# A searched order, sums and stores for pairs of token tiles, and an early sine in a fused FFN and long-convolution kernel

**Chip, cores, metric.** One core of a Trainium2 chip. Time is the device time of one execution in microseconds (us). The kernel before takes 190.48 us (median of 3 runs, 189.39 to 190.49).

## The reference

Input is x (2048 tokens by 640), k and v of the same shape, a 4-tap filter, a long filter of 2048 taps for each channel, and a feed-forward network (FFN) of width 1728. The result is x + s * g:

```python
def _A_ref(q, k, v, shift_k, ssm_k, ssm_D):     # s: a long convolution
    ...                                         # k_shift: 4 taps along the tokens
    kv = k_shift * v
    ...                                         # kv_f, kf_f: FFTs over 2*S samples
    y = ...                                     # irfft(kv_f * kf_f)[:S]
    y = y + kv * ssm_D[None, None, :]
    return q * y

def _B_ref(x, w1, b1, w2, b2):                  # the FFN
    h = _gelu(jnp.einsum("bsd,df->bsf", x, w1) + b1)
    return jnp.einsum("bsf,fd->bsd", h, w2) + b2

xn = _layernorm(A_q)
s = _A_ref(xn, A_k, A_v, A_shift_k, A_ssm_k, A_ssm_D)
g = _silu(_B_ref(xn, B_w1, B_b1, B_w2, B_b2))
return A_q + s * g
```

## The kernel before

The transforms are matrix products on TensorE. The first stage writes to DRAM (scrK, scrU). Twelve convolution units (six for each half of the channels) read a block of k and of u back, do the second stage, multiply, do the inverse's first stage into the tile of u, and store it (scrC). FFN matmuls fill the time between. All operations are listed once with what they depend on; a string, ORDER, gives the order in which they are issued, the engine of each (p TensorE, a ScalarE, d VectorE, g GpSimd, s SyncE's DMA queue) and the slot of each buffer.

```python
    def finish(j):                              # one token tile: sum and store
        op("fin", "DVE", lambda e: eng(e).tensor_tensor(out=xs(j), in0=xn[:, j, :], in1=xs(j), op=ALU.add),
           reads=[xn_b[j]], writes=[x_b[j]])
        op("store", "SP", lambda e: nc.sync.dma_start(out=out_v[:, j, :], in_=xs(j)), reads=[x_b[j]], size=160 * 1024)
    # ...
    uin_pool = Pool(vA_t + vB_t, [[vA_h]] * 2 + [[vB_h]] * 2)      # four tiles for u
    # ... in conv_unit(b, u):
        chain("uin", op("uin", "SP", lambda e: rd(scrU, uin), reads=scrU_b[b], writes=[uin], size=P * n * 2, extra=last("uin")))
        # ... s2k, s2u: second stage (L723); s2ev: evictions (L265); prod, comb: products on VectorE
        op("i1", "PE", i1, reads=[qb, tab_b], writes=pc)           # inverse, first stage (L755)
        # ... i1ev: evicted into uin.v
        op("cst", "POOL|SP", lambda e: dma(e)(out=by_n2(scrC)[:, b, k0:k1, :],
                                                        in_=uin.v[:, 0:n].rearrange("p (k d) -> p k d", d=H)),
           reads=[uin], writes=[scrC_b[b][u]], size=P * n * 2)
```

Unit 7's u can be read only when unit 3's result, which lies in the same tile, is stored. Other lines: L513 is the FFN's first product (f1), L576 its second (f2), L580 its silu, L610 the first transform stage, L777 the inverse's last stage, L559 the output store. In the changed kernel the numbers are 2 to 8 higher (L515, L584, L588, L618, L731, L763, L785, L564), and by one more where an experiment adds a line.

## Time and profile before

| | before (profiled execution) |
|---|---|
| span | 189.8 us |
| TensorE busy | 176.4 us (93%) |
| first real FFN matmul | 10.88 us |
| unit 3's, unit 6's, last unit's inverse | 116.8, 136.7, 160.4 us |
| last matmul, and the time from it to the end | 185.05 us, 4.75 us |

The rows to read are those of TensorE, which bounds the kernel: how much of a stretch it stands idle, what it waits for, and what clock it was granted. The prediction below shows these lines.

### The profile page before, as it was taken

The numbers are of one execution on the slowest core, as the hardware profiler recorded it, in microseconds if no ns is written. First come the engines' busy times: TensorE is split into PE (matmuls) and PEld (weight loads), VectorE is DVE, ScalarE is ACT, GpSimd is POOL, SyncE is SP. The second block draws the span as 40 slices with busy tenths as digits, with TensorE's granted clock in tenths as the row PEclk, the third lists the DMA queues.
The fourth block names the chain that finished last, engine by engine and source line by source line (L and its number), as shares of the span: only waits on it lengthen the run. The fifth ranks groups of instructions, "written<-read, shape, count | busy, mean of one in ns | idle before, by whom it ended". The sixth has DMA issues, their size and how long they took to land.

```text
span 189.8 us, 4770 instructions
## 1 busy us (share of the span) xinstructions
PE 176.4 (93%) x1907; PEld 92.2 (49%) x1907; DVE 164.6 (87%) x302; ACT 146.5 (77%) x225; POOL 20.6 (11%) x35
## 2 busy tenths in 40 slices
PE   7899999999898899999999999985999999989990
PEld 2285543345554465656433444332246565646660
DVE  6799979994799999999989999996498998669993
ACT  2899799797986999999999999994599987111110
POOL 4470410031021030000001100110010000000000
PEclk9999999999999999999999999996699999999997
DMA  5999969999999987898699998879762999568375
GB/s 141 350 418 414 408 200 348 323 310 379 384 333 328 234 282 206 155 293 252 137 298 286 243 380 256 240 192 327 215 207 50 342 303 337 157 214 338 107 260 191
DMA packets 44410, 51.44 MB, mean 271 GB/s; under 512 B 7442, under 2 KB 38547, under 8 KB 44388
## 3 DMA queue, kind: packets, MB, share of 16 engines
q1 hardware_dynamic: 43216, 47.03, 77.8%
q0 software_dynamic: 1024, 4.10, 6.4%
q8 instruction: 15, 0.25, 0.6%
q14 instruction: 7, 0.06, 0.1%
q10 hardware_dynamic: 148, 0.01, 0.1%
HBM read 31.47 MB, written 18.35 MB: 262 GB/s over the span
## 4 chain that ended last, share of the span: by engine, by line
PE 45%; DMA 29%; DVE 17%; ACT 4%; issue 2%; SPq 1%; POOLq 0%; ACTq 0%; DVEq 0%
PE ps L513 18%; PE ps L576 14%; DMA scrC<-v_all 9%; DMA mm<-scrC 7%; DMA kT<-in_x_dram 4%; PE ps L610 4%; DMA scrK<-mm 3%; PE ps L723 3%; DVE stats L383 3%; DMA v_all<-scrU 3%; DVE xn L784 2%; DMA x<-in_x_dram 2%; ACT mm L265 2%; DVE kT L557 2%; PE ps L777 1%
## 5 line engine op out<-in xcount | busy, mean ns | idle before, releaser
L513 PE MATMUL ps<-xnT,w_sb 128*128 128x512 bf16 (+1 forms) x280 | 64.5, 379 | 0.9 <-ACT sl L580 0.5
L576 PE MATMUL ps<-w_sb,hT 128*128 128x320 bf16 x432 | 63.6, 300 | 0.5 <-ACT sl L580 0.5
L576 PEld LDWEIGHTS <-hT 128*128 128x128 bf16 x448 | 41.8, 98 | 21.6 <-issue 5.8
L265 ACT CAST mm<-ps 128x640 bf16<-128x640 f32 (+1 forms) x62 | 39.4, 703 | 4.4 <-DMA scrK<-mm 3.3
L513 PEld LDWEIGHTS <-w_sb 128*128 128x128 bf16 x280 | 26.6, 101 | 31.4 <-issue 8.9
L265 ACT CAST v_all<-ps 128x960 bf16<-128x960 f32 (+2 forms) x38 | 33.4, 916 | 6.4 <-PE ps L723 4.1
L519 ACT ACTIVATE hT<-ps,b_f 128x512 bf16<-128x512 f32 (+1 forms) x56 | 36.9, 706 | 1.7 <-PE ps L513 1.2
L580 ACT ACTIVATE sl<-ps 128x320 bf16<-128x320 f32 x32 | 13.6, 445 | 21.1 <-PE ps L576 18.8
L784 DVE TENSOR_TENSOR xn<-ps,xn 128x640 bf16<-128x640 f32 x16 | 12.6, 817 | 3.8 <-PE ps L777 3.0
L736 DVE TENSOR_TENSOR kT<-v_all,k_all 128x960 bf16<-128x960 bf16 x16 | 9.8, 652 | 4.2 <-ACT v_all L265 4.2
L723 PEld LDWEIGHTS <-tabs 64*32 64x32 bf16 x704 | 7.6, 92 | 11.7 <-issue 7.3
L635 DVE TENSOR_TENSOR mm<-k_all,mm 128x2560 bf16<-128x2560 bf16 x8 | 11.8, 1480 | 0.1
L632 DVE TENSOR_TENSOR mm<-k_all,mm 128x2560 bf16<-128x2560 bf16 x8 | 11.8, 1478 | 0.0
L723 PE MATMUL ps<-v_all,tabs 64*32 64x240 bf16 (+1 forms) x352 | 9.0, 274 | 2.9 <-DMA v_all<-scrU 2.9
L265 DVE CAST v_all<-ps 128x960 bf16<-128x960 f32 (+1 forms) x8 | 8.6, 1070 | 2.1 <-PE ps L755 1.0
L383 DVE BATCH_NORM_STATS2 stats<-kT 128x6 f32<-128x320 bf16 x16 | 6.9, 472 | 3.8 <-DMA kT<-in_x_dram 3.8
L610 PEld LDWEIGHTS <-W 64*128 64x128 bf16 x128 | 4.5, 94 | 10.7 <-issue 8.0
L736 DVE TENSOR_TENSOR k_all<-v_all,xtra 128x960 bf16<-128x960 bf16 (+1 forms) x16 | 9.0, 609 | 0.1
L390 POOL TENSOR_TENSOR rstd<-veps,mhalf 128x4 f32<-128x4 f32 (+1 forms) x5 | 6.2, 1235 | 23.6 <-DVE veps L388 23.6
L265 ACT CAST k_all<-ps 128x960 bf16<-128x960 f32 x8 | 7.8, 977 | 0.4 <-PE ps L723 0.4
L582 DVE TENSOR_TENSOR xn<-xn,sl 128x640 bf16<-128x640 bf16 x16 | 7.7, 483 | 0.1
L265 DVE CAST k_all<-ps 128x960 bf16<-128x960 f32 x6 | 6.9, 1154 | 1.0 <-ACT v_all L265 0.8
(98 smaller groups left out, 200.7 us busy)
## 6 DMA issues: line engine op xcount, KB each, us to landing
mm<-scrC SPq DMA_DIRECT2D x8, 640.0 KB, 5.5
v_all<-scrU SPq DMA_DIRECT2D x10, 480.0 KB, 4.9
scrK<-mm SPq DMA_DIRECT2D x12, 320.0 KB, 3.8
scrU<-mm SPq DMA_DIRECT2D x12, 320.0 KB, 3.6
k_all<-scrK SPq DMA_DIRECT2D x7, 480.0 KB, 5.8
scrC<-v_all SPq DMA_DIRECT2D x7, 480.0 KB, 4.9
kT<-in_kT_dram SPq DMA_DIRECT2D x4, 640.0 KB, 10.6
v_all<-in_v_dram SPq DMA_DIRECT2D x4, 640.0 KB, 8.4
```

The costliest lines, as they stand in the source:

```text
L265: (nc.scalar.copy if e == "ACT" else nc.vector.tensor_copy)(out=out_, in_=in_)
L383: nc.vector.bn_stats(out=stats[:, j, h, :], in_=xs(j)[:, h * H:(h + 1) * H])
L513: nc.tensor.matmul(out=ps.v[:, lo * P:hi * P], lhsT=w1_sb[:, ft, t, :], rhs=xnT_b[c].v[:, t, lo * P:hi * P], start=(t == 0), stop=(t == DT ...
L519: op("gelu", "ACT", lambda e: nc.scalar.activation(out=hT_b[c].v[a:z, ft, :], in_=ps.v[a:z, :], func=ACT.Gelu_apprx_tanh, bias=b1_f[a:z, f ...
L576: nc.tensor.matmul(out=ps.v[:, 0:H], lhsT=hT_b[c].v[0:M, ft, q * P:(q + 1) * P], rhs=w[:, h * H:(h + 1) * H], start=(ft == 0), stop=(ft == ...
L580: op("silu", "ACT", lambda e, h=h, ps=ps: nc.scalar.activation(out=sl.v[:, h * H:(h + 1) * H], in_=ps.v[:, 0:H], func=ACT.Silu), reads=[ps ...
L610: nc.tensor.matmul(out=ps.v[:, h, 0:H], lhsT=W[r, j + t, :], rhs=src[r, b, j + t, :], start=True, stop=True)
L632: op("kv2", "DVE", lambda e: tt(out=kt_t, in0=win(0, 2), in1=wbc(0, 2), op=ALU.mult), reads=kb + [wb_b], writes=[kvt_b], extra=[u for b in ...
L635: op("kv2", "DVE", lambda e: tt(out=kt_t, in0=win(2, 2), in1=wbc(2, 2), op=ALU.mult), reads=kb + [wb_b], writes=[kvt_b])
L723: nc.tensor.matmul(out=ps.v[32 * g:32 * g + 32, r, i * w:(i + 1) * w], lhsT=F2[i][64 * r:64 * r + 64, :], rhs=part(src.v[64 * r:64 * r + 6 ...
L736: nc.vector.tensor_tensor(out=q[:, r], in0=uu[:, r, :, None, :].to_broadcast([P, 2, 2, w]), in1=ku[:, r, None, :, :].to_broadcast([P, 2, 2 ...
L784: nc.vector.tensor_tensor(out=xv, in0=ps.v[:, :, 0:H], in1=xv, op=ALU.mult)
```

## The change

The intent: fewer and larger sums and stores at the end, one activation-table load fewer at the start, and an order found by a search whose model had transfer times fitted to measured ones.

```diff
+NPAIR = 12
 ORDER = """
-1d 7p0 9s 1s 1s 1s -18p1 10g 1g -6p0 -7d 48d -27s 1s ...
+2d 5p0 -3p1 11a 53p0 -50s 1s 1s 1s 1s 5s 42a -58p1 -11d ...
 (the whole string is another one)
+    op("presin", "ACT", lambda e: nc.scalar.activation(out=acs[:, CH - 1, 0:1], in_=bias_pi[:], func=ACT.Sin), reads=[bias_b])
 ...
-    op("small2", "DVE", small2, writes=[sm_b], after=stat_ops)
+    op("small2", "DVE", small2, writes=[sm_b], after=stat_ops[:3])
 ...
-    def finish(j):
-        op("fin", "DVE", ...)
-        op("store", "SP", ...)
+    def finish(j, n):
+        x_, xn_, b = (xs2(j), xn[:, j:j + 2, :], x_b[j:j + 2]) if n == 2 else (xs(j), xn[:, j, :], [x_b[j]])
+        op("fin%d" % n, "DVE", lambda e: nc.vector.tensor_tensor(out=x_, in0=xn_, in1=x_, op=ALU.add), reads=xn_b[j:j + n], writes=b)
+        op("store", "SP", lambda e: nc.sync.dma_start(out=out_v[:, j:j + n, :] if n == 2 else out_v[:, j, :], in_=x_), reads=b,
+           size=n * 160 * 1024)
     def step_done(j):       (a pair is finished when both its tiles are)
```

In the new order, unit 3's store is also issued by SP where the old one had GpSimd's queue.

More of the change, by code (lines that the diff above doesn't have):

```diff
@@ L132 @@
 ORDER = """
-1d 7p0 9s 1s 1s 1s -18p1 10g 1g -6p0 -7d 48d -27s 1s 9d 1d 1d -24p1 -4p0 9a 23a -31p1 28g 5d -1d 2d 1g 3g 21p0 -2p1
--28d 1d 28a -22d 1d 6d 1d 17p2 -51g 52a -7p3 1a -38s -14p4 -7p5 63a -41s -14p4 -7p1 65p2 -46s 47a 22d -47d 27s 12p10
-2p0 2p2 -3a 2a 3p1 -1a -60s 62a -76d 36a 60p00 -18d -41a 200d 1d -227s 69d -1d 2d -13s 14g -51a -19s 227d 1d -142p3
--15d -70s 73d 11p2 4p 4a 9p1 -6p4 7a 9p5 -24p -16d 18p 2a 5a 13p6 -37d 14p2 13p1 11a 2a -12a -26d 23p0 60p60 1a 1p4
--113s 52a -8p -88s 92a 9p1 57a -53p0 -14a -48s 117p61 2p4 -3s 4a -2a -55a 120d -153p21 1d -24s 25p3 1d 3p4 -38d 39a
@@ L138 @@
--3p5 1d 24a 73p62 -25p23 1a 25d 51d -124p0 49p4 25p6 -24a 17p20 8a -133s 119g 7a -67a 75s -68p10 2p4 -1a 2a 1p5 50p61
-2p2 5p0 -43p4 109d 1d 1d 1d -75a 2a 5a -122s 80p6 -1a 10p22 2p0 -26a 11p4 115d 12d -122a 22s 15s -26a -91s -5s 90p5 4a
-3g 1p63 -17a 115d 12d -27p01 28d 1d 1d 1d -121a 132d -123p2 73s -72a -2a -100s 183a 42d -152p4 273d -271p2 270d -271a
-270d -273p3 5a 108p6 -91a 92a 29p02 -142a 31g 112a -126p2 1a 214p40 -78d 121d -41p5 -1a 2a -91p6 -82p03 2p2 81a -89g
-181p41 -123s 41d 121d -213a 24p60 149d -147p0 -24a 91d -9p21 -44s 212d -77a -148a 56s 251s1 -120g -189a 69d -91s 82a
@@ L143 @@
-91p5 -148s 149a -91p0 -18p62 2p2 17a -220s 202a 2a 1s 107p40 -74d -10p03 156d -163s 92a 73d -157a 256s0 -300p60 2p2 1a
-160d 3d -37p5 -128a 3g -104p4 145p0 3p22 78d -115p61 43d 110a 4s0 -38a -84a -34a 37a -159p5 165d 143d -142d -164p0
-155s 10d -156a 112p6 37p2 -36a 37a -158a 309d -144d -167a -75s 316p11 2p4 -119g 118a 70g -72d 4a -83s -100p60 30p23 1a
-182d 4s -27p00 -189a 190a -74d -92p41 2p2 191s -186p6 -4a 303s0 -116d -97d 134d -219a -201d 202s 220d -70d 1p11 71d
--137d -93a 227a -133d 137s1 -136d -116p22 -3p6 5p4 -1a 186p0 -189a 252d 77p2 2p6 -326a 178a 7a -60d 205p4 -216d 12d
@@ L148 @@
-60d -350p1 1d 164s 324a -146p0 73s 79a -204d 200a 1d1 13s1 -339p23 330p4 10p6 -162a 1d -53d -125a 189p10 141a 1d -313s
-322a -8d -142a -189p2 1a 324d -200d -122p42 2p6 121d 121s -255s 198p0 150p2 -334a 240s -242a 187a -54d 204a -9p64 2a
--1a -150p01 161p2 2p4 -235p61 73a -46d 47p1 160a 2a -235a 1p2 229d0 -156a -47d -44p40 2p6 17a -16a 250d -346s 247p00
-16p1 89s1 -227p23 2p6 -33d 154a 85s -128s 142d -221a 123p4 -111d 112a 91d -77a -58p00 -201s 349p2 -147a -79d -31s
-251p46 1a -210d 120p1 96a -242s 27d 120a 93s0 -3d -122p0 1a -100s 17p42 -5p60 7p2 203s -127p1 -77d 209p4 -207d 221s2
@@ L153 @@
--228a 215d -227p61 95a -93p2 -1a 2a 87p0 1a -71g 208d1 13s1 -228p6 -45p43 2p2 -1a 45d 215d -92p1 -166a 259p4 2p6 10p2
--162p0 178s0 -120a 95a 10a -12d 3d -250p42 2p6 -1d 96a -94a 109p1 1a -82g 244s2 -24d -541p0 550p2 1a -241s 244p6 2p4
--1d 27s1 -304s 279a -556d 448p1 1a 92p26 1a 9d2 1d -9a -93a -157s 272p4 -121p0 1a 112d -164p2 -4p3 178p6 4p0 -5d 7p4
--15d -164a -391p2 569d 10s3 -192a 178a -171p3 172d0 -565a 555p60 15a -13a -115p2 98s -146a 185p4 2p0 8s2 -146a 139a
--2a -24d 34s0 1p6 -20d -184p3 179d -8g 14d -216d 32a 219s0 -181p2 157d1 -10p04 1d 10d 8a 16s1 -33a -196p3 197g -149a
@@ L158 @@
-166p6 4p4 -3a 5p0 1a -220a 245s1 -242p2 243s2 -28d -3d2 1d 5d -16p64 2a -159p0 158a -202a 225p4 -180a 182p6 1a 3p2 1a
--180p1 152s 29p6 -185p0 186a -181a 173d -8d 25p4 16s2 -30d0 6d 25s3 -211a 170p26 25a -227p1 204a -1d -202a 22p0 1a
-204p4 4p2 2p6 -638p1 425p0 208a -10d -14g 30a -22d 20d 27s0 -238a -425d 633d1 6d -16p42 -174p61 176a -1a 23p0 2p2 4p4
--203a 200a -199p7 197d -8d 15p0 -292d 301s0 -13d2 -25s 28a -202a 204a 25s1 -47d 23d 8p2 1a -8d -204p60 -1d 250s0
--62p40 1d 25p2 15s1 -39a 25a 1d0 -213p7 215p0 -216a 218p2 10p4 -11a 26s1 -46d -188p61 210a 1d 33s2 -24a -227a 1d 235s3
@@ L163 @@
--49s 15p02 1a 10d 15p4 1a -25a 15d -210p7 1a 220d1 1d -11p04 2d -214a 197s -178p20 205p64 -11a 2s 14p0 -3a -1d 5d
--227d 18p3 1a -2a 211p4 1d 4p6 10p0 1d -20s 34s3 -24d -214d -9p31 1a 224p4 2p0 -7p6 -240p20 241d 9p6 -2d -2d 22p0 6p4
--5d 24s0 -23d 5d -274a 250d 21d 4d 4s1 -2d -276p2 1a 1d 250s2 -232p3 278p0 -19p4 6p6 -277p20 291d -24s -254a 248s
--247d 249s 9d 6d 16d -15d -4d 1s -31p0 6p4 18s 15p6 -4s 12d 1s -41d 43s -22d -271p3 244d 7d -6d 1s 1d 25s 7d 1s
--277p41 280d -284a 254d 1s -6s -244a -3a 1d 282d -32s 33s -280p2 1a 1d 279d 1s
+2d 5p0 -3p1 11a 53p0 -50s 1s 1s 1s 1s 5s 42a -58p1 -11d 13g -5p2 1p1 -8a 48d -24s 39p0 -32d 1d -21p1 -2p2 -7p1 62a
@@ new lines @@
+-27a -24g 48p2 -28d 6d -5g 4d 27p0 -25d -5d -30p1 10d 26g 25a -43s 13d 26a 13s -6p3 1a -66p1 38d 1d 1g -22s 27d 1d -5d
+50d -70s 68d -9p20 8d -6p3 -14s 13a 3p0 2p1 -3a 2a 22p20 -20a 21p3 -18d -42a -1a -5a 50d 35p0 -34g 155d -137p -17d 18p
+137d -121a -12a 15p1 -107s 99p4 -8a 17a 3p5 -2p6 1a -111s 2s 96p0 1a 14a -11p7 1a -57s 132p20 -5p01 6a -104d -1d 100d
+-78p6 -10p5 15a -52s 38p7 93p2 -83a -50s 101p02 33a -109d 4p41 1a 72a -69p6 102s -126s 94p2 -69a -8d 154d 1d -184d 46p
+4a -16p4 73a 1s 77d -150d 151d 11d -159p0 9p 4a 11p1 47p23 -98s 120p4 -92a 159d 1d 1d 1d 12d -102p6 -1a 22a 1g 69d
@@ new lines @@
+-90a 102d 1d 1d 1d 12d -159p00 -7a 50s -168g 143p2 -78s 61a 18a 5p3 25p40 -24a 26p6 -7p02 -24p2 32a -2a -44p3 -67s
+106a -24a 33p61 2p4 -34p0 -15a 50a -31p1 29a -32a 23p2 23p43 2p6 -55p0 37g 17a -62p4 19a 20a -19a 44a -70p5 56s -29p20
+2p6 -142s 128a -7p1 -1a 23a -2a 209p00 2p4 -238a 70s 75d 12d 1d 1d -114s 115d 1d -153a 99s 39p61 -32p23 123a -121p0
+56d -25a -30a 124p51 -150p62 24a 33p0 -118s 143d 66a 3a 78d -171a 91d 3p4 -108p20 -43a 82d -68s 171d -344s 311a -69d
+-57s -25p0 44p6 -1a 140d -30p50 71d -167s -56a 185d -141a 263s1 -154a 71d -151p23 -16p01 2p6 -250d 251a -59s -180p4
@@ new lines @@
+224s 139d 2d -32p5 -80a -252a 253p6 -50p22 33a -31p0 128a 70d -74d -75a -169p4 -67s 221g 7p60 159d -199a 42p0 117g 41g
+-151s -6d -45a 299s0 -408p5 152a -154p2 167d -46p61 2p0 191d -200s 65d -22s -164a 10a 239p31 2p4 -120a -2a 151d -148g
+-48p03 238d -314a 91p62 225a -149d 73d 78s0 -139d -254s 348d -93d 62a 2a 148s0 -147d 70d -223a 185s1 -31p20 -169a 104d
+-120p40 5p61 251d -239p0 198d -25p31 -4a -185a 120d 1d -116a 254s -242a -16p4 5p6 206a -22a -58d 126s -227p0 1a -30a
+1s 183p2 -179a 180a -169s 115d 198p0 2p4 4p6 -5a -141p3 -3d -54d 200a 1d1 13s1 -10a -146a 147p0 10p4 -13d 4a -307s
@@ new lines @@
+166p20 151a -93s -57a -7d 148d 1d -333p60 113p03 -111p4 1a 111a 71p31 149p40 1a -131d -78d -125d 335a 20s1 -170a -59d
+81s -21p2 -59d 81s -21a -356p4 1a 306d 203p6 4p0 -3a 4a 1p2 -4d1 -152p5 157a -220p62 1a -126s 189a 165p0 -8d -99p40
+94d 6d -236p2 244a -228p6 1a 75s 48p5 82s -221d 94p00 42a -253s 353p62 22s0 -118a -116d 214a -213d 70a 142d -220s
+128p1 1a -34p4 -213p20 2p6 117p01 133p5 -38a 128s0 -168d -47d -126a 339g -238g -99a 117d 59d -97p22 2p0 37p6 -117s
+249a -168d 37a 116p4 -155a 45d -313p5 314d 216p0 -222g 116a 110p6 2p2 -5a -84p4 -176s 266a -536d 534d 10s1 -230p03
@@ new lines @@
+247s2 -113a -55p5 54a -132d -28p20 2p6 105a -75p01 -29a 241d1 -148p4 -95d 244d -211p6 -5p2 4a -49p02 20s 93a 11p5
+-123a 1p0 49d 240s2 -25d -220a 228p6 2p2 -151a -122a 160p4 114a -2d -228g 117a 116p0 2p6 -15d 25p2 -11d 2a -116p5
+111d2 -10p06 2d 9d -275s 289a -161p4 162p2 -25a 29p0 2p6 -16d -116a -116s 256s1 -23d 24s3 -138p5 124a 1d0 3a -28s 30a
+-185p2 186d -130a -42p3 156p06 -153a -2a -17p4 206s0 -23d -142p3 132a -170a 204s0 -206a 173d 15d -14s 21p0 2p6 10p4
+16s2 -27d -150p2 152d 10a -9d1 25s1 -613p0 578p46 2d -150a -28p1 34a 143a 19p2 -597a 402a 186d 13p4 2p6 -5d 1d2 3a 2a
@@ new lines @@
+1d -163p0 164d -223p1 206p24 -146a -59a 207a 22p6 -23a -144p0 168a -34g 35p4 4p2 10s1 -29d 16d 5p6 -230p1 226d0 -25s
+-145a 175a -229p0 227a -13p46 11d -188p2 178d 22s2 17s0 -255a 2a 215a 14d 8p0 17s3 -16a 1p6 4p4 1a -14d -193a 203d
+-183p31 159s -158a 173p04 2d -1a -173p2 186p6 10p4 2p0 -197a 181d1 -179p30 184d -4d 5d 11a -2a 3d2 -196a 198p6 10s2
+-9a 1p0 10p4 -1s0 -211d 173s 30a -16d 26a -210p2 211p6 4p0 2p4 -16d 11d 1d0 12s1 17s0 -26a 10s1 -24d -201a 7p31 210a
+-22d -194d 225p0 10s1 10s2 -28d -34p64 67s3 -24a -8d -34a 1a -177p2 204d -205a 220p0 1a -42s 15p64 -192a 194a -1a 27d1
@@ L168 @@
+-25s -178p30 1a 192p04 11d -202p2 193a -1d -191a -19d 221p64 2d -1a -10s -192d 206p0 10p2 2p6 -11d -3s -213p41 1a 227d
+-2d 17s2 -11p0 -2p6 -228p5 215p2 14d 2d -11p6 -219a 217p0 -216d -24p40 238d 30p2 -27d 2d 21p0 -262p5 270s3 9s1 -4p6
+-8d -268a 272p2 -270a 262d 23p0 -278p41 256d 4d 8d -24s0 1p6 19d 15d -285d 7a 279d -11d 1s -21p2 8s 15p0 -7d 8d
+-268p40 1a -4p5 264s -16d -4d 15s -10d 30s -29s -5d -244a 245s -244d 270d 1s -268p4 275d 1s -275a 1d 267d 1s
 """
@@ L554, with xs2 @@
     left = {}
-    def finish(j):
-        op("fin", "DVE", lambda e: eng(e).tensor_tensor(out=xs(j), in0=xn[:, j, :], in1=xs(j), op=ALU.add),
-           reads=[xn_b[j]], writes=[x_b[j]])
-        op("store", "SP", lambda e: nc.sync.dma_start(out=out_v[:, j, :], in_=xs(j)), reads=[x_b[j]], size=160 * 1024)
-    def step_done(j):
-        left[j] = left.get(j, 3) - 1
-        if left[j] == 0:
-            finish(j)
+    def xs2(j):
+        return x01[:, j:j + 2, :] if j < 2 * CH else x23[:, j - 2 * CH:j - 2 * CH + 2, :]
+    def finish(j, n):
[3 more added lines that the diff above has]
+           size=n * 160 * 1024)
+    def step_done(j):
+        j0 = j - j % 2 if j < NPAIR else j
+        n = 2 if j < NPAIR else 1
+        left[j0] = left.get(j0, 3 * n) - 1
+        if left[j0] == 0:
+            finish(j0, n)
     def f2(c, q):
```

## The prediction

> **What bounds the kernel now.** I first read the page's busy times with the slices, then TensorE's waits, then the timeline round the longest wait, then the chain of waits, and last VectorE's timeline at the end.
>
> ```profile
> span 189.8 us, 4770 instructions
> ...
> PE 176.4 (93%) x1907; PEld 92.2 (49%) x1907; DVE 164.6 (87%) x302; ACT 146.5 (77%) x225; POOL 20.6 (11%) x35
> ...
> PE   7899999999898899999999999985999999989990
> ...
> PEclk9999999999999999999999999996699999999997
> ```
>
> TensorE (PE) is the bound: 176.4 of 189.8 us busy, and the change removes no matmul. So it can gain only in what is not full-speed matmul work: some 13 us without work, and the stretch where the clock row falls to 6, in the 28th and 29th slice (of 4.75 us each, so from 128 to 138 us). TensorE's own waits say where:
>
> ```profile
> PE ps L723 <- DMA v_all<-scrU: 2.9, 1, 2.9
> PE ps L311 <- DVE xtra L305: 1.3, 1, 1.3
> PE ps L777 <- DMA mm<-scrC: 1.2, 2, 0.8
> PE ps L610 <- DVE v_all L639: 0.9, 1, 0.9
> ```
>
> One wait of 2.9 us stands out: the second-stage transform (L723) waits for a block of u that is read back from DRAM into a tile of v_all. TensorE's timeline there:
>
> ```profile
> 127.20 0.40 PE L723 MATMUL ps<-k_all,tabs 64*32 64x240 bf16 x16
> 130.45 0.60 PE L723 MATMUL ps<-v_all,tabs 64*32 64x240 bf16 x16 [2.85 <-DMA v_all<-scrU]
> ...
> 131.38 2.32 PE L513 MATMUL ps<-xnT,w_sb 128*128 128x512 bf16 x5
> ...
> 134.16 2.26 PE L513 MATMUL ps<-xnT,w_sb 128*128 128x512 bf16 x5
> ...
> 137.22 1.04 PE L513 MATMUL ps<-xnT,w_sb 128*128 128x512 bf16 x4
> ```
>
> After it the groups of five L513 matmuls take 2.25 and 2.19 us in the chain where others take 1.13 to 1.19. So the wait costs twice: 2.85 us idle, then about 2 x 1.05 + 0.8 (the L723 groups) = 2.9 us of slow clock. What led to the wait is in the chain:
>
> ```profile
> 117.65 1.16 DVE v_all L265
> ...
> 118.84 0.48 issue
> ...
> 119.33 5.93 DMA scrC<-v_all
> ...
> 125.32 5.08 DMA v_all<-scrU
> ...
> 130.45 1.00 PE ps L723 x25
> ```
>
> There are four tiles for u. Unit 3 of the convolution writes its result over its u, stores it (5.93 us, from the POOL queue), and only then may the u of unit 7 be read into the same tile (5.08 us). From the start of unit 3's first inverse transform (116.84 us) to the u of unit 7 it is 13.6 us, and the order gives TensorE less than that to do.
>
> [...]The trace has eight loads of 1.28 us; at 12.03 us the sine activation starts right behind its load (13.32 us)[...]. [...]additions of 640 bf16 elements take 0.48 us and follow each other by 0.40 to 0.43, those of 1280 take 0.82 and follow by 0.69 to 0.73. [...]The output stores of 160 KB land after 1.9 to 2.2 us[...].
>
> **The change part by part.** *Sums and stores for pairs.* Tiles 0 to 11 are summed and stored two at a time: 16 sums become 6 of 1280 elements and 4 of 640, and 16 stores become 10. VectorE saves 12 x 0.42 - 6 x 0.72 = 0.7 us, and SP six issues of 0.33 to 0.5 us. All of it is after 171 us, where VectorE hardly rests (7.70 of 8 us in the stretch 172 to 180) and stays a step behind TensorE. The last links stay, for the last tile is still single:
>
> ```profile
> 185.73 0.48 DVE L582 TENSOR_TENSOR xn<-xn,sl 128x640 bf16<-128x640 bf16 x1
> 186.25 0.49 DVE L557 TENSOR_TENSOR kT<-xn,kT 128x640 bf16<-128x640 bf16 x1
> ```
>
> TensorE ends at about 185.1 us and the kernel at 189.8: silu, product, sum and the last store keep these 4.7 us. I count 0.3 us for less VectorE backlog.
>
> *Sine table first.* A one-element sine is put ahead of the first statistics on ScalarE. [...]the load at 12.03 us goes: 1.28 us of ScalarE. But TensorE does not wait for ScalarE between 11 and 22 us (11.00 of 11.00 busy[...]), so this shortens a backlog and not the end. The new order puts one or two evictions of the weight rows before ScalarE's statistics, in time it now waits for x (2.21 us), of the five between 7.11 and 9.53 us, so the transposes' evictions and the first real matmul (10.88 us) may come 0.3 us earlier. If instead the load sits behind the first of these evictions it delays the statistics by about as much. I count 0.3.
>
> *Order.* I counted the blocks of work on TensorE in both orders, and priced them from the trace (L513 group 1.14, L576 group 2.01, L723 group 0.33, inverse 0.61, L465 group 0.33). From unit 3's inverse to unit 7's u, the old order has six L513 groups, seven L723 groups and three inverses: 6 x 1.14 + 7 x 0.33 + 1.5 = 10.7 us. The new one has seven L513 groups and one L465 group besides: 12.1 us. And unit 3's store moves from the POOL queue to SP, without the 0.48 us of issue and nearer the 4.9 us median of SP's stores: the need falls from 13.6 to about 12.5. So the wait falls from 2.85 to about 0.5: gain 2.3 us. With it the slow clock should go in most runs. In the profiled execution it cost 2.9 us; but that one took 191.6 us, and the three timed ones had a median 1.1 us below, so part of the spell was often absent: I take 1.3.
>
> Earlier, VectorE stood 3.78 us on the late second half of x before its statistics, and TensorE waited for it (the 0.9 above). The new order holds these statistics until more products of k and v are done: gain 0.9.
>
> Against this, new tight spots. From unit 4's inverse to unit 8's u the work stays 12.2 us, while the need is 12 to 13.6, and its store is still on POOL; before, the stall of unit 7 fell inside this stretch and covered it. The first tile of v's second half is free only 5.7 us of work before unit 4 needs its u, against 0.4 us of issue and the 4.9 us median landing. Units 9, 10 and 11 have 13.1, 13.4 and 14.5 us (13.7, 14.3 and 14.8 before). At the end, three L576 groups and the inverse transforms still cover about 9.3 us between the last unit and the first read of its results; so the 0.8 us wait there stays. I charge 1.0.
>
> Sum: 0.3 + 0.3 + 2.3 + 1.3 + 0.9 - 1.0 = 4.1 us; 190.48 - 4.1 = 186.4.
>
> **The rivals.** First, *the wait is moved, not removed*: unit 8, or unit 4, or the stores of the first half (ScalarE waits 3.3 us on scrK stores now) stop TensorE for 2 to 3 us, perhaps with another slow spell. For it: DMA is over 90% busy in many slices, and landings of one kind vary (the reads of scrU from 3.1 us up), so an order tuned to mean landings can miss. Against it: all four covers but the one named stay within 0.9 us of the old. That makes 188.5 to 190.5. Second, *the slow clock is a matter of phase*: any idle time can bring it, or the fast runs of before never had it. Then only idle time counts: 187.5 to 188. Third, *VectorE becomes the bound*: with TensorE some 4 us faster, VectorE's 164.6 - 0.7 us must fit into a shorter span (about 88%), and it follows rather than leads between 104 and 120 us, where it is already full (7.85 and 7.99 of 8 us). Against it, what it loses now (3.78 us for x, some 4 us round the big wait) comes back. That would make 187. A better case: with no wait left in the middle and no slow spell, 6 to 7 us fall, to 183.8.
>
> **Range and chances.** The limit of 2% is 186.67 us, close to my 186.4. The gain is one wait with its slow clock; if both go I am well under, if the order moves the wait I am over. There is nearly nothing that could cost 2%. I give 0.53 to faster, 0.45 to same and 0.02 to slower, and 183.8 to 189.4 as the range.
>
> **What would show it.** Right: TensorE's longest wait for v_all<-scrU under 1 us, the clock row without a 6, L513 groups of 1.2 us throughout, seven table loads and none at 12 us with the time at the first L513 matmul near 10.6, VectorE without a stop for x near 48 us, a busy time of VectorE lower by about 0.7 us, and TensorE's busy time lower by 1 to 3 us for the missing slow spell. Wrong: a new wait over 2 us of TensorE on scrU, scrC or ScalarE, a clock that falls anyway, or a start of the first L513 matmul after 11.5 us.

## The result, and the profile after

The changed kernel took **183.88 us** (median of 4 runs: 188.76, 183.26, 184.08, 183.69), the kernel before in the same rounds 190.49. The ratio is 0.964, with an interval of 0.956 to 0.972: faster. Ratios here are the mean time of one kernel's fast runs over that of the other's fast runs of the same rounds, so not quite the ratio of the medians. The profiled execution happened to be the slow one of the four. Its page, answering to the rows of before:

```profile
span 187.0 us, 4730 instructions
...
PE 174.6 (93%) x1894; PEld 92.4 (49%) x1907; DVE 165.7 (89%) x296; ACT 146.6 (78%) x226; POOL 17.8 (10%) x33
...
PE   6999999999999999999999999994999999996990
...
PEclk9999999999999999999999999998599999999999
```

The low clock is still there, in the 29th slice (0.50 from 129.4 to 136.2 us), behind a wait of the same kind. TensorE's timeline in that execution:

```profile
130.09 0.60 PE L731 MATMUL ps<-v_all,tabs 64*32 64x240 bf16 x16 [2.52 <-DMA v_all<-scrU]
...
131.82 4.05 PE L515 MATMUL ps<-xnT,w_sb 128*128 128x512 bf16 x9 [0.34 <-issue]
```

A second execution of the same file was profiled in the fast state (span 183.0 us; experiment a_again):

```profile
128.65 0.40 PE L731 MATMUL ps<-v_all,tabs 64*32 64x240 bf16 x16 [1.85 <-DMA v_all<-scrU]
...
129.39 2.33 PE L515 MATMUL ps<-xnT,w_sb 128*128 128x512 bf16 x10
```

Read the two together: the wait for unit 7's u is there in both, 2.52 and 1.85 us, where I had expected 0.5. Behind it, nine matmuls took 4.05 us in the one, ten took 2.33 us in the other. (The x1894 of the page says that 13 matmul records are missing in that trace; the 0.34 us of "issue" goes with such a gap.) So the wait was made smaller but not removed, and the slow clock comes behind it in some executions only. Why the wait stays is in the chain of the first of the two:

```profile
116.18 0.62 PE ps L763 x16
...
118.86 5.70 DMA scrC<-v_all
...
124.58 5.46 DMA v_all<-scrU
```

From unit 3's inverse at 116.18 to the u of unit 7 at 130.04 it is still 13.9 us (13.3 in the fast execution, 13.6 in the profile of before). The store is on SP now, but took 5.70 us all the same, and it was issued no sooner after the inverse: 2.75 us behind the inverse's start (2.49 before). The timeline shows what it waited for:

```profile
117.33 0.40 DVE L753 TENSOR_TENSOR kT<-kT 128x480 bf16<-128x480 bf16 x1
...
117.64 1.15 DVE L266 CAST v_all<-ps 128x960 bf16<-128x960 f32 x1
...
118.86 0.36 SPq L774 DMA_DIRECT2D scrC<-v_all  x1
```

VectorE evicts half of the inverse's result. It was still at two sums of 0.40 us (L752, L753) when the inverse ended at 116.72, so its eviction ended only at 118.79, 0.07 us before the store. (The chain names two gelus of ScalarE at this point; the second ended at 118.95, after the store's issue, so it was not they.)

What became better lies elsewhere. The rows of time by stretch give, for each stretch, its length and the busy time of TensorE, then of weight loads, VectorE, ScalarE and GpSimd. Before:

```profile
34.00:50.00 16.00, 15.32 (x98) 7.28 (x96) 11.91 (x16) 14.21 (x24) 2.09 (x3) 1.00 0.98 347
50.00:64.00 14.00, 12.58 (x93) 7.08 (x91) 13.76 (x30) 11.53 (x21) 1.88 (x2) 1.00 0.97 321
```

And in the fast execution of after:

```profile
34.00:50.00 16.00, 16.00 (x107) 7.86 (x105) 15.59 (x16) 14.86 (x25) 0.69 (x1) 1.00 0.97 329
50.00:64.00 14.00, 13.61 (x100) 7.36 (x97) 13.69 (x36) 12.71 (x22) 2.73 (x3) 1.00 0.98 326
```

VectorE is busy 15.59 of 16 us where it was 11.91, and TensorE's idle time in the two stretches falls from 2.10 to 0.39 us. VectorE's stop in the timeline of before has no counterpart after:

```profile
48.53 0.89 DVE L383 BATCH_NORM_STATS2 stats<-kT 128x6 f32<-128x320 bf16 x2 [3.78 <-DMA kT<-in_x_dram]
```

The 6.8 us between the two profiled spans (189.8 and 183.0) split, by TensorE's idle time in each stretch and the length of its matmul groups, as follows: 2.9 the slow spell of before; 1.1 less wait between 120 and 131 us; 1.8 less idle from 22 to 64 us; 0.7 in 112 to 120 and 152 to 163; 0.85 at the start (next paragraph); minus 0.5 in 163 to 172 us, before the inverse's last stage; minus 0.2 from the last matmul to the end (5.0 against 4.8 us); the remaining 0.2 I don't place.

The start: in the first 11 us TensorE's idle time fell by 0.5 us, but its first FFN matmul came only 0.05 us earlier (10.83 and 10.88). What counts is when the clock becomes full. The first matmuls of 256 columns follow each other by 0.213 us up to 13.4 us in the profile of before, and by 0.109 from there; in the fast execution of after the step comes at 11.7 us. That is 1.7 us less at half speed. It differs between executions of one file, too (13.4 in the slow profile of after), so it is no merit of the change.

The early sine did not save a load. ScalarE's timeline after:

```profile
2.03 1.28 ACT L266 ACT_TABLE_LOAD   x1 [2.03 <-issue]
...
3.93 1.28 ACT L304 ACT_TABLE_LOAD   x1
```

The first eviction loads a set, and the sine behind it loads its own; the load at 12.03 us is gone, so there are eight as before. The first L515 matmul begins at 10.89 us (10.83 in the fast execution; 10.88 before).

### The profile page after: what moved, and what is told of

Same layout as the page of the kernel before. It is cut to its first block, busy times and chain, and to the rows that moved or that the text cites. A ratio compares the mean times of both kernels' runs of the same rounds, so it can differ in the third digit from the quotient of the medians.

```text
span 187.0 us, 4730 instructions
## 1 busy us (share of the span) xinstructions
PE 174.6 (93%) x1894; PEld 92.4 (49%) x1907; DVE 165.7 (89%) x296; ACT 146.6 (78%) x226; POOL 17.8 (10%) x33
## 4 chain that ended last, share of the span: by engine, by line
PE 69%; DMA 16%; DVE 7%; ACT 4%; issue 1%; SPq 1%; ACTq 0%
PE ps L584 28%; PE ps L515 21%; DMA w_sb<-in_w_dram 6%; PE ps L731 5%; PE ps L618 5%; DMA scrC<-v_all 3%; DMA v_all<-scrU 3%; PE ps L763 3%; DVE xn L792 3%; DMA mm<-scrC 3%; PE ps L313 2%; ACT mm L266 2%; DVE kT L563 2%; DVE x L563 2%; PE ps L480 1%
## 5 line engine op out<-in xcount | busy, mean ns | idle before, releaser
L515 PE MATMUL ps<-xnT,w_sb 128*128 128x512 bf16 (+1 forms) x267 | 62.6, 379 | 1.7 <-issue 1.1
L515 PEld LDWEIGHTS <-w_sb 128*128 128x128 bf16 x280 | 26.2, 102 | 31.6 <-issue 9.1
L266 ACT CAST mm<-ps 128x640 bf16<-128x640 f32 (+1 forms) x60 | 38.9, 709 | 2.2 <-PE ps L618 0.9
L266 ACT CAST v_all<-ps 128x960 bf16<-128x960 f32 (+2 forms) x32 | 28.8, 922 | 4.7 <-PE ps L731 3.2
L588 ACT ACTIVATE sl<-ps 128x320 bf16<-128x320 f32 x32 | 14.2, 449 | 21.5 <-PE ps L584 21.5
L266 DVE CAST v_all<-ps 128x960 bf16<-128x960 f32 (+2 forms) x14 | 15.1, 1082 | 6.4 <-PE ps L763 3.0
L266 ACT CAST k_all<-ps 128x960 bf16<-128x960 f32 x12 | 11.9, 988 | 1.0 <-PE ps L731 1.0
L744 DVE TENSOR_TENSOR k_all<-v_all,k_all 128x960 bf16<-128x960 bf16 x16 | 9.7, 652 | 1.4 <-ACT v_all L266 1.4
L618 PE MATMUL ps<-v_all,W 64*128 64x320 bf16 x64 | 7.8, 300 | 0.0
L266 DVE CAST mm<-ps 128x640 bf16<-128x640 f32 x9 | 7.4, 820 | 0.1
L744 DVE TENSOR_TENSOR kT<-v_all,k_all 128x960 bf16<-128x960 bf16 x12 | 7.2, 653 | 0.2
```

What stands on the lines that cost most here:

```text
L266: (nc.scalar.copy if e == "ACT" else nc.vector.tensor_copy)(out=out_, in_=in_)
L515: nc.tensor.matmul(out=ps.v[:, lo * P:hi * P], lhsT=w1_sb[:, ft, t, :], rhs=xnT_b[c].v[:, t, lo * P:hi * P], start=(t == 0), stop=(t == DT ...
L588: op("silu", "ACT", lambda e, h=h, ps=ps: nc.scalar.activation(out=sl.v[:, h * H:(h + 1) * H], in_=ps.v[:, 0:H], func=ACT.Silu), reads=[ps ...
L618: nc.tensor.matmul(out=ps.v[:, h, 0:H], lhsT=W[r, j + t, :], rhs=src[r, b, j + t, :], start=True, stop=True)
L744: nc.vector.tensor_tensor(out=q[:, r], in0=uu[:, r, :, None, :].to_broadcast([P, 2, 2, w]), in1=ku[:, r, None, :, :].to_broadcast([P, 2, 2 ...
```

## The experiments

In the order texts below, "f1#44" is the 45th operation of kind f1, and so on. Before took a median of 189.8 to 190.4 us in each of the five batches.

### Both kernels again

Edits: none.

> The kernel before, unchanged, to see the granted clock of each of its runs. Theory A (one wait of TensorE near 2.9 us for unit 7's u, and the slow clock it brings, make most of the change's gain): every run near 190.5 us has a mean clock near 0.98, that is, the slow spell is in all of them. Rival P (the slow clock is a matter of phase, and the kernel before has it as rarely as the kernel after): some runs have a clock of 1.00 and take about 187.5 us.

> The kernel after, unchanged. Theory A: most runs take 183.3 to 184.1 us at a clock of 1.00, and a run that has the slow spell again shows a clock near 0.98 and takes about 5 us more, near 188.8, because the wait and the spell come together. Rival P: clock and time are not tied; there are runs at 0.98 of 185 to 187 us.

b_again: 190.13 us (15 runs from 187.41 to 192.11, and two of 335 and 581 us that I leave out here; the median is over all 17), ratio 1.001. a_again: 184.57 us (184.07 to 186.61), ratio 0.971. Both are what they were. Theory A fails for the kernel before: its clocks reach from 0.959 to 0.997 in these runs, and in the same rounds one run at 1.000 took 189.33 us, where rival P had 187.5. For the changed kernel no run near 188.8 came; the one slow run, 186.61 at 0.988, lies where rival P put it. In b_again's profile TensorE waits 3.6 us for u; in a_again's it waits 1.9.

### Is it the wait for unit 7's u?

b_cover moves two groups of L513 in front of the wait, b_fill puts 12 useless matmuls there (their result is overwritten):

```diff
 order of before (b_cover)
+f1#44 (TensorE), f1#42 (TensorE)
 s2u#13            the one that waits for unit 7's u
 ...
-f1#44
-f1#42
```
```diff
 before (b_fill)
-                def s2(e, src=src, ps=ps, t=t):
+                def s2(e, src=src, ps=ps, t=t, fill=(nm == "s2u" and b == 1 and u == 1 and t == 0)):
+                    for _ in range(12 if fill else 0):
+                        nc.tensor.matmul(out=ps.v[:, 0, :], lhsT=w1_sb[:, 0, 0, :], rhs=flat(w1_sb[:, 0])[:, 0:512], start=True, stop=True)
```

> The kernel before with only this: two groups of five L513 matmuls (2.3 us) that followed the wait for unit 7's u now stand ahead of it. Theory A: the wait falls from 2.9 to about 0.6 us, the slow spell goes, clock 1.00: 190.5 - 2.3 - 2.9 = about 185.3 us. Rival R (the gain comes from the pairs, the table and VectorE's order, spread over the kernel): 189 to 190. Rival G (given back: what was moved is missing behind the wait, and TensorE stops there instead): 187.5 to 189.

> The kernel before with twelve needless 128x512 matmuls (12 x 0.216 = 2.6 us at full clock) into the bank of unit 7's first product, just ahead of it, so that the array works while the u is awaited. The wait for the u is not shorter. Theory A: no slow spell, clock 1.00, time falls by the spell alone, 2.9 us: about 187.6. Rival P (the spell isn't due to the idle time): clock still near 0.98, time 190.5 or a little more.

b_cover: 188.53 us (19 runs, 187.43 to 191.74); its ratio of fast runs, 0.999, says "same". b_fill: 188.80 us (4 runs, 186.07 to 189.61), ratio 0.982. In b_cover the wait for u fell to 0.23 us, but TensorE then stood 0.87, 0.26 and 0.47 us right behind it: the matmuls moved up were missing there. In both profiles the span was 186.2 to 186.3 us, with no slow spell. So the wait with its spell is worth some 3.5 us in an execution that has both, but only about 1.5 us in the median, for executions without the spell are common in the kernel before too. It alone doesn't make the change.

### A fifth tile for u

The table W of sines is needed for the last time by its four transposes (gtr). When all are done early, its memory can hold one more tile of u, and unit 7 need not wait for unit 3's store:

```diff
-    uin_pool = Pool(vA_t + vB_t, [[vA_h]] * 2 + [[vB_h]] * 2)
+    W_h = held([W_b])
+    uin_pool = Pool(vA_t + vB_t + [flat(W)[:, 0:UC]], [[vA_h]] * 2 + [[vB_h]] * 2 + [[W_h]])
 order: the last gtr and its eviction some 30 to 90 operations earlier; uin#7 into the new tile right behind uin#6;
 uin#8 to uin#11 each at the place of the one before
```

> The kernel after with a fifth tile for u: the weights W of the first stage are needed no more once they are transposed, so unit 7's u goes there at once, and each later u takes the tile that its forerunner had (the last W transposes moved ahead to free it). Theory A (reuse of the u tiles makes the wait): TensorE's wait of 1.9 us for unit 7's u goes to under 0.3, none of that kind takes its place, and no slow spell is seen: about 184.6 - 1.9 = 182.7 us. Rival G (given back: the products behind it or the read of the results stop TensorE for as long): 184 to 184.6.

> The kernel before with the same fifth tile and nothing else (the last W transpose moved ahead). Theory A: the wait of 2.9 us and the slow spell, found in about half of its runs, go: 190.1 - 2.9 - 1.3 = about 186 us, clock 1.00. If the order does the rest of the change's gain elsewhere, it stays 1 to 2 us above the kernel after (184.6). Rival G, as it was with the two groups moved: 188 to 188.5.

a_fifth: 183.63 us (182.60 to 183.88), ratio 0.969; no wait for u is left in TensorE's list. But of the 1.9 us only some 0.5 to 0.9 reached the end: the run lies between theory A's 182.7 and rival G's 184, and TensorE now waits 0.7 us for a block of k (L732) and 0.6 us for ScalarE (L467). b_fifth: 189.33 us over 16 runs (185.86 to 191.80), ratio of fast runs 0.985. The old order gains little in the median: its clocks still reach from 0.971 to 1.0, though the profiled execution had neither the wait nor a slow spell (184.2 us). What brings the low clocks in its other runs is not shown: none of them was profiled.

### The statistics alone

VectorE's stop for x, taken away in the old order: the statistics that wait go behind the last product of that part.

```diff
 order of before (b_stats)
-stats#9, stats#8, stats#7, stats#10, veps#3, pow#3 at their six places
 kv1#15
+stats#9, stats#8, stats#7, stats#10, veps#3, pow#3
```

> The kernel before, with only the statistics of the four tiles 8 to 11 moved back on VectorE, behind the next products of k and v, as the new order has it. If VectorE's 3.8 us stop for x at 45 to 48 us is worth what I predicted: VectorE has no stop for x, TensorE's waits near 58 us go, and the time falls by 0.9 to 1.8 us, to about 188.8. Rival: the wait further on takes it all up (TensorE only comes earlier to unit 7's u): within 0.4 us of the kernel before.

194.20 us (3 runs, 191.39 to 194.82), ratio 1.019, with an interval from 0.999 to 1.039: no gain, and probably slower. TensorE's waits show what took its place:

```profile
PE ps L513 <- ACT sl L580: 3.3, 1, 3.3
PE ps L723 <- DMA v_all<-scrU: 2.8, 1, 2.8
```

VectorE now waits 3.4 us for ScalarE and 2.2 us for x anyway, and TensorE stands 3.3 us for ScalarE with a slow spell behind (the mean clock of this execution is 0.973). So VectorE's stop can't be removed by that move alone, and the run doesn't tell what the stop itself cost.

### The pairs and the early sine

a_noparts has the new order with single sums and stores and no sine; a_nopairs has the sine; b_parts is the old order with both parts.

```diff
 after (a_nopairs)
-NPAIR = 12
+NPAIR = 0
 (a_noparts) as well:
-    op("presin", "ACT", ...)
 before (b_parts): the code of after, the old order, presin#0 ahead of asum#0 on ScalarE, each pair where its second tile was
```

> The kernel after in its own order, but without the other two parts: sums and stores tile by tile, each pair's in the place of the joint one, and no early sine. Theory O (the order makes the gain): 184.6 + 0.7 = 185.3 us at most. Rival R (pairs and table are worth 2 us or more): over 186.6.

> The changed kernel with its pairs undone and its early sine kept. Undoing both cost 2.0 us. Theory S: the pairs are most of it, through the seven single stores that SP issues one after another: 185.6 to 186.4 us, and 6.0 to 6.3 us from the last matmul to the end. Rival T (the early sine is most of it, by a faster start): 184.6 to 185.2, and about 5 us at the end.

> The kernel before with its old order, and only the two coded parts of the change: sums and stores for pairs, and the sine of one element ahead of ScalarE's first statistics. Theory S (the pairs only pay where SP's issues of the last stores end last, which they do in the new order and not in the old; ScalarE's early load is off the path): 189.3 to 190.3 us, ratio 0.993 to 1.003, time from the last matmul to the end 4.6 to 4.9 us. Rival P (the two parts are worth the 2 us that they were worth in the new order, whatever the order): 187.8 to 188.5, ratio 0.986 to 0.990.

a_noparts: 186.57 us (185.46 to 188.34), ratio 0.983. a_nopairs: 185.98 us (184.70 to 186.29), ratio 0.982. b_parts: 191.53 us (190.15 to 192.01), ratio 1.012, although its early sine did leave out a table load (seven in its trace). So the parts give nothing in the old order (if anything the reverse; three runs), and in the new order the pairs give most of what both give; between a_noparts and a_nopairs, with overlapping ranges, the sine shows no gain that three runs could settle. Where the pairs gain is seen in SP's timeline at the end of a_noparts (second column: time over all the issues of the group):

```profile
180.18 1.89 SPq L564 DMA_DIRECT2D out_dram<-x  x4
182.16 1.40 SPq L564 DMA_DIRECT2D out_dram<-kT  x3
```

and SP's of a_again:

```profile
178.15 1.83 SPq L564 DMA_DIRECT2D out_dram<-kT  x3
```

In a_noparts SP issues seven stores one behind the other, 0.47 us each, and is done at 183.56, 1.59 us after the end of VectorE's last sum (181.97). With pairs it is done at 179.98, 0.45 us after that end (179.53). From the last matmul to the end it is 6.2 us in a_noparts, 6.0 in a_nopairs and 4.5 to 5.0 in the four profiles of the changed kernel (4.8 before). In the kernel before, SP is 0.6 us behind VectorE (187.35 and 186.74) without any pairs, so there was nothing to gain. By the traces the pairs are worth 1 us or more, in SP's issues and not in VectorE's sums, and only where the order brings the last sums close together: they take back what the new order itself loses at the end. (The times of three runs each, from other rounds than the changed kernel's, would not show it by themselves.)

### Half of the order each

Up to about 66 us both orders have done nearly the same set of operations. h_early takes the new order (without the two parts) up to there and the old one for the rest, h_late the reverse.

```diff
 h_early: operations 1 to 315 of the new order, then what is left in the old order
 h_late:  operations 1 to 309 of the old order, then what is left in the new order
```

> A graft: the new order (without pairs and early sine) for the first 315 operations, up to some 66 us, then the old order for all that is left. Theory E (the gain of the new order in the first 64 us goes through to the end): TensorE idle 0.6 us or less between 22 and 64 us against 2.45 in the kernel before, the wait for unit 7's u stays near 3 us with the slow clock in part of the runs, 188.0 to 188.9 us, ratio 0.987 to 0.992. Rival M (the later DMA round trips set the time, and what comes early is waited away later): wait for unit 7's u over 4 us, 189.6 to 190.6 us.

> The opposite graft: the old order for the first 309 operations, then the new order (without pairs and early sine). Theory E (the middle is worth what its smaller wait and the missing slow spell give, 1.0 and about 1.5 us): 187.2 to 188.4 us, ratio 0.983 to 0.989, no slow spell, 6 us from last matmul to end. Rival (the new order gains only through its first 64 us): 189.6 to 190.6 us. A second rival (the whole gain is in the middle): 186.3 to 186.9, which is the changed kernel without its parts.

h_early: 189.57 us (19 runs, 188.31 to 190.84), ratio 1.001. h_late: 191.63 us (19 runs, 188.83 to 194.22), ratio 1.005. Neither half brings anything. For h_late the graft itself spoils the test: TensorE waits 1.9 us at the seam for ScalarE, the first transform stage ends at 110.4 us in place of 106.7, the wait for u is 2.9 us as before, and the clock in its profile is low a second time, from 8.2 to 11.6 us. h_early is clearer: TensorE's idle time from 22 to 64 us was 0.66 us (2.45 before), and unit 6's inverse came at 131.5 us (136.7 before, with the slow spell). But then:

```profile
147.31 0.60 PE L723 MATMUL ps<-v_all,tabs 64*32 64x240 bf16 x16 [2.43 <-DMA v_all<-scrU]
147.84 3.48 PE L576 MATMUL ps<-w_sb,hT 128*128 128x320 bf16 x14
```

A later u is waited for, and a slow spell follows (14 matmuls in 3.48 us; 2.08 is the full speed). This is rival M, at another unit than I had named. If it is so, the fifth tile must bring the early saving to light:

```diff
 h_early
+ the fifth tile for u, as in b_fifth  (h_fifth)
```

> The graft with the new order's early half and the old rest, plus the fifth tile for u. The early half brought TensorE to unit 6's inverse 5.2 us earlier than in the kernel before and it then lost 2.4 us waiting for a later u, with a slow spell behind it. Theory E (the early saving is real and was waited away): no wait for u over 0.5 us, no slow spell, ratio 0.972 to 0.980 (185 to 186.5 us), clearly under the old order with the fifth tile (0.985). Rival M (something else behind the convolution sets the end, the early saving is lost anyway): 0.985 to 0.990.

185.69 us (185.30 to 186.84, all clocks 0.997 or more), ratio 0.978. TensorE at the same place:

```profile
145.54 0.40 PE L724 MATMUL ps<-v_all,tabs 64*32 64x240 bf16 x16
145.87 2.08 PE L576 MATMUL ps<-w_sb,hT 128*128 128x320 bf16 x14
```

Theory E fits: the early saving is real, and it reaches the end when the tiles of u do not hold it back. Neither the fifth tile in the old order (189.33) nor the early half alone (189.57) is worth more than 1.1 us in the median; together they are worth 4.2. One caution: the profiled executions of b_fifth and h_fifth are alike (184.2 and 184.0 us), so a good part of the difference is that h_fifth's executions are all good ones; and the ratios of fast runs, 0.978 and 0.985, have intervals that still touch (0.973 to 0.983 and 0.980 to 0.990).

### One letter: the store of unit 3 on SP

```diff
 order of before (b_sp)
-cst#3 on GpSimd's queue
+cst#3 on SP
```

> The kernel before with one letter changed: unit 3's store goes from the POOL queue to SP. As predicted (no 0.5 us of issue, and a landing nearer 4.9 than 5.9 us): the wait for unit 7's u falls from 2.9-3.6 to 1.5-2.4 us, the slow spell is rarer, 188.0 to 189.3 us, ratio 0.989 to 0.996. Rival (the landing depends on what else is under way and not on the queue): wait 2.7 us or more, 0.998 to 1.003.

188.32 us (8 runs, 185.75 to 190.33), ratio 0.986. The store is issued at 118.59 us and the read of u 5.04 us behind it; before it was 119.33 and 5.99:

```profile
118.59 0.36 SPq L766 DMA_DIRECT2D scrC<-v_all  x1
123.63 0.36 SPq L706 DMA_DIRECT2D v_all<-scrU  x1
```

The wait for unit 7's u is gone in this profile; units 8 and 9 wait 0.8 and 1.6 us in its place. So this step of the prediction was sound in the old order, and larger than the 1.1 us that I gave it. In the change the same letter gained less: its store took 5.16 to 6.24 us in the four profiles of the unchanged file, and VectorE's eviction ahead of it ended 2.7 us after the inverse's start, where it was 2.0 before.

### How often is the slow spell there, and a version without it

To see whether the changed kernel's slow executions are chance, it was run again, beside a version with the fifth tile and the sine ahead of ScalarE's first eviction:

```diff
 a_fifth
+first#0 (VectorE) right behind zero#0, presin#0 ahead of wbev#3   (a_best, a_best5)
 after, unchanged                                                  (a_more, a_more5)
```

> The changed kernel once more, unchanged, as the measure for the version with the fifth tile in the same rounds: 183.9 to 184.8 us, ratio 0.967 to 0.973.

> The changed kernel with the fifth tile for u, and the one-element sine moved ahead of the first eviction on ScalarE, so that one table load should be left out (seven in place of eight). The fifth tile alone gave 183.6 us. If ScalarE's load at 3.93 us is off the path: 183.3 to 183.8; if the statistics behind it are on it: up to 0.5 less, 183.0. Seven loads in either case.

> The changed kernel, unchanged, in five rounds. If the slow clock behind the wait for unit 7's u comes by chance in about half of the runs: some runs near 184.0 us at clocks of 0.997 or more and some near 187.3 us at 0.99 or less, none far from both. Rival (the slow group belonged to one chip or one hour): all of one group.

> The changed kernel with the fifth tile for u and the sine's load first, in the same rounds. With no wait for a u no slow spell can follow it: all runs at clocks over 0.99 and between 182.9 and 184.3 us, median 183.7; seven so far were. Rival (the slow clock comes for other reasons): a third to a half of the runs near 186.5 us.

a_more: 187.24 us (185.78 to 188.00), ratio 0.985. a_more5: 184.25 us (183.93 to 186.58), ratio 0.977. a_best: 183.89 us (182.90 to 184.05), ratio 0.966. a_best5: 184.22 us (183.27 to 185.26), ratio 0.975. a_best5's forecast was too narrow: two of its six runs (184.39 and 185.26) lie above 184.3 us, and one clock is 0.986, at 184.18 us. The miss of a_more (expected 183.9 to 184.8) told more than a hit would have. Its timeline:

```profile
129.25 0.45 PE L731 MATMUL ps<-v_all,tabs 64*32 64x240 bf16 x16 [1.96 <-DMA v_all<-scrU]
...
130.44 3.52 PE L515 MATMUL ps<-xnT,w_sb 128*128 128x512 bf16 x10
```

With a wait of 1.96 us the ten matmuls took 3.52 us; in a_again, with 1.85 us, 2.33. All executions of the changed kernel (three batches and the first measurement), of the kernel before in the five batches, and of the two versions of after with the fifth tile:

| kernel | granted clock | runs | mean us | from, to |
|---|---|---|---|---|
| before | all | 127 | 190.10 | 187.10, 194.04 |
| after | all | 18 | 185.31 | 183.26, 188.76 |
| after | 0.997 or more | 11 | 184.12 | 183.26, 184.74 |
| after | 0.989 or less | 7 | 187.17 | 185.78, 188.76 |
| after with the fifth tile | all | 13 | 183.84 | 182.60, 185.26 |

The changed kernel has two groups with nothing between them, 3.05 us apart in the mean. That is not one spell of fixed length: in the three profiles of the upper group it cost 2.9 us (after), 1.6 (a_more) and 1.4 (a_more5), by the time from the u of unit 7 to the end of unit 6's inverse against a_again; the wait ahead of it and a later full clock at the start make up most of the rest. No run of the version without a wait for u is in the upper group. Both groups came within two batches (one run of four in a_again, one of six in a_more5), so it is no matter of chip or hour alone; but all four runs of a_more are in it, so the share of 7 in 18 isn't sure.

A pattern that fits these profiles can be read from the clock of the traces, cut into stretches of 3.4 us. In the clock records of before and after, the changes lie 116.05, 6.83 and 51.20 us apart, which is 34, 2 and 15 times 3.413 us. The slow spells of b_again, a_more and a_more5 are one such step long (b_again's clock of 0.81 in 131 to 140 us is 3.4 us at half). Where this grid falls differs from execution to execution (first change at 13.4 us in before, 11.7 in a_again). Before, and then the fast execution of after (each row: the stretch, its length, the busy time of the engines, and then TensorE's clock, 1.00 or 0.50):

```profile
126.00:129.40 3.40, 1.57 (x21) 0.52 (x20) 3.37 (x7) 2.38 (x5) 0.00 (x0) 1.00 1.00 264
129.40:132.80 3.40, 2.35 (x36) 1.07 (x37) 1.59 (x5) 1.68 (x2) 0.00 (x0) 0.50 1.15 323
```
```profile
124.40:127.80 3.40, 2.39 (x40) 0.80 (x38) 3.05 (x7) 3.40 (x7) 0.00 (x0) 1.00 1.02 270
127.80:131.20 3.40, 2.56 (x57) 1.42 (x58) 1.94 (x3) 1.74 (x3) 0.00 (x0) 1.00 1.15 333
```

In the first, 1.8 us of the wait lie in one stretch, and the next one runs at half the clock. In the second the grid cuts the wait in two halves of 0.9 us, and nothing happens. The other profiles agree:

| run | wait for unit 7's u | the most of it in one stretch | slow spell behind it |
|---|---|---|---|
| before | 2.85 us | 1.8 us | 6.8 us |
| after | 2.52 us | 1.8 us | 6.8 us |
| b_again | 3.59 us | 2.3 us | 3.4 us |
| a_more | 1.96 us | 1.96 us | 3.4 us |
| a_more5 | 2.47 us | 2.0 us | 3.4 us |
| a_noparts | 3.09 us | 1.7 us | none |
| a_nopairs | 1.99 us | 1.5 us | none |
| a_again | 1.85 us | 0.9 us | none |

The longest waits of b_parts, b_stats, h_early and h_late have 2.0 to 2.9 us in one stretch, and each has a spell behind it (five matmuls of L515 in 2.31 us in b_parts, ten of L513 in 3.30 in h_late, fourteen of L576 in 3.48 in h_early, where 1.25, 2.33 and 2.08 are the full speed; b_stats has a mean clock of 0.973). So, in these traces and after the first 14 us, a stretch with 1.8 us or more of one wait brought the half clock and one with 1.7 or less did not; once low, the clock stayed low for a second stretch when that one had 1.0 us or more without work (before, after, b_stats). No run was made to test this; it is read from the traces afterwards. It also means that the mean clock of a run is a rough measure, for it counts the low clock of the last microseconds too, where TensorE has no work left (0.50 from 187.4 to 189.8 us in before, whose last matmul ended at 185.05).

In a_best TensorE goes through the place without a stop:

```profile
128.83 2.33 PE L515 MATMUL ps<-xnT,w_sb 128*128 128x512 bf16 x10
```

a_best has seven table loads (the set loaded for the sine at 2.03 us served the evictions, statistics and sines behind it up to the next load at 14.93 us) and is no faster for it than a_fifth (183.63). The fifth-tile version beats both kernels: by 6.3 us before, and by 1.5 us on average after, mostly by being rid of the slow group.

## Why the prediction was right or wrong

The prediction was 186.4 us with 183.8 as its low end; the ratio of the first measurement, 0.964, is 183.6. The direction and the class were right, the size was too small. Step by step:

- **What bounds the kernel.** Right: TensorE's idle time and its clock account for nearly all of the 6.8 us between the profiles.
- **The wait for unit 7's u, 2.85 to 0.5, gain 2.3.** This is the step that failed in its mechanism, and the largest of the sum. The wait stayed at 1.85 to 2.5 us in the four profiles of the changed file: gain 0.3 to 1.0. The need was put at 12.5 us; it measured 13.3 to 14.2. The store's 4.9 us was a median of all stores of SP, and this one took 5.16 to 6.24, a spread wider than the 0.5 us that was to be left of the wait; and the 0.5 us saved at the issue were lost again because VectorE did two sums ahead of its eviction (store issued 2.75 us behind the inverse's start, 2.49 before). The cover was put at 12.1 and was 11.5 us (115.3 to 126.8 in the fast profile).
- **The slow clock, 1.3.** Half right. The spell did not go: it is in three of four profiles, at 1.4 to 2.9 us each, and 7 of 18 executions are of the slow group. So the prediction's "clock row without a 6" failed. Nor does every wait near 3 us set it off: a_noparts had one of 3.09 us and no spell. Between the profiles of before and a_again the term is 2.9 us, 1.6 more than I counted; that much is the luck of the grid.
- **VectorE's stop for x, 0.9.** This is the term whose size failed, and it made the total too small. The stop of 3.78 us is gone. But I priced it by one wait (0.87 us, for v_all), and TensorE's idle time between 22 and 64 us fell from 2.45 to 0.61 us: 1.8 us. Not all of that is the stop's. Of the 2.45 us, 0.87 and the 0.55 at 62.45 us (ScalarE there had waited for VectorE) can come from it; 0.51 at 49.73 us is ScalarE's, which had waited 1.21 us for a scrK store and then loaded a table, and the rest lies before the stop. That the order, and not the statistics alone, brought the 1.8 us is shown by h_early (0.66 us idle); that the stop was its cause is not shown. Two further stretches gave 0.7 us that no term of mine named (round 112 and 152 us).
- **New tight spots, minus 1.0.** Too much: only the wait before the inverse's last stage grew, by 0.5 us.
- **Pairs, 0.3.** Wrong engine: 1 us or more against the new order without them, through SP's issues of the last stores, but nothing against the kernel before, for the order had lost as much at the end. I had listed the six issues saved and then counted only VectorE. "The last links stay" overlooked that SP is one of them.
- **Sine first, 0.3.** Wrong, as the text's own "if instead" foresaw: the load sits behind an eviction, eight loads remain, and the start did not move. With seven (a_best) nothing is gained either, which fits that ScalarE's backlog is not on the path there.

The terms without the spell come to 2.8 us by the prediction; runs of clock 0.995 or more took 189.3 us before (mean of 21) and 184.1 after, which is 5.2. The profiles place only about 3 us of that (without the spell and the start), so some 2 us of the gain have no named cause (the start's 0.85 may be part of them). What lies above 5.2 in the first measurement is chance: of the first four executions three were of the fast group. All 18 have a mean of 185.31, inside the range; a single number between two groups, 184.1 and 187.2, was bound to be far from most runs.

Of the rivals, "the wait is moved" did not happen in the change, but it did in h_early, b_cover and b_sp. "The slow clock is a matter of phase" was right, as far as the profiles show: a spell came or not by how the grid of 3.41 us cut the wait. What sets the grid's place at the start of an execution stays open.

What else stays open: the split between the order's early and late half in the change itself, since h_late's seam spoiled it; the 2 us without a name; and whether the sine has any effect within 0.5 us.

## What to carry to other kernels

A saving at the start of a kernel is real only if no later round trip (here: result stored, tile read again) holds it back; try it together with one buffer more before calling it worthless. Price an order by all the idle time of the bound engine in a stretch, and follow each gap to what ended it: one wait (0.87 of 2.45 us here) is not the whole, and neither is the whole due to one cause. When the clock drops in some executions only, look at where its changes fall in the trace before calling it chance. And when executions fall in two groups, predict the groups and their shares: four runs can't tell 3.6 per cent from 2.5.
